# Smaller first loads, last stores on two queues, and a new order of loads and units in a fused attention and GEGLU kernel

## The chip, the cores and the metric

The kernel runs on one core of one Trainium2 chip. The metric is the device time of one execution in microseconds, where lower is better. Times of several executions are given by their median.

## The reference

```python
def _attn_ref(q, k, v):                       # each [8, 12, 448, 64], float32
    S = q.shape[2]
    scale = 1.0 / np.sqrt(q.shape[-1])
    scores = scale * np.matmul(q, k.transpose(0, 1, 3, 2))
    attn = np.maximum(scores, 0.0) ** 2 / S
    return np.matmul(attn, v)

def _moe_ref(x, w_gate, w_val, w_out):        # x [3584, 768]; w_gate, w_val [768, 1536]; w_out [1536, 768]
    g = x @ w_gate
    gelu = 0.5 * g * (1.0 + erf(g / np.sqrt(2)))
    return gelu * (x @ w_val) @ w_out
```

The attention has a squared ReLU in place of the softmax, so there is no sum over a row. Its output, with the heads side by side, is the `x` of the second part. The result is [3584, 768] in float32.

## The kernel before

**Stages.** For each of the eight batches q, k and v come in by DMA from POOL, converted to bf16 on the way. q and k are turned so that the head dimension lies on the partitions: on TensorE for batches 0 and 1 and one third of batch 2 (`add_transposes`, L676), by DMA transposes on SP for the rest (`add_dma_transposes`). A score unit (`add_scores`) makes scores for two heads at a time; ACT applies the ReLU while it empties the PSUM bank (L743), and DVE squares (L752). `add_values` multiplies by v, and the result is `xT`. The gate and value products come either as plain units (`add_gate_value`: a gate or a value for one batch and 128 columns of the 1536) or, for pairs of batches, in a scheme of seven products in place of eight (`add_pair`). Their GELU times value is `uT`. The last product, with w_out, also goes in seven products for a group of four chunks of 64 rows by two tiles (`add_product`); there are 14 groups, 0 to `FINAL` = 13, and each makes two output tiles `osb` of 128 rows. When both column halves of a tile have been read out of PSUM, its two halves of 64 rows are stored with one DMA each.

**The array.** Nearly all matmuls use a quarter of TensorE (64 rows by 64 columns). Two streams, `PE0` for the upper rows and `PE1` for the lower ones, run side by side, each with two column halves.

**The order.** All instructions are put in order before the launch by `run_plan`, which walks a model of the engines with a cost for every step and emits each step when the model starts it. Up to the first gate unit the order of TensorE is fixed by numbers in the code. After that the units stand in a list, written out in `LINE`: a token of one character is the next item of a kind (`s` scores, `o` values, `0` to `7` plain gate or value of that batch), `0E3` is product 3 of the pair of batches 0 and 1 in column block E, and `n2` is product 2 of output group n (13). `next_unit` looks at the first 60 entries and takes the first whose inputs are there. So `LINE` gives preferences. `LOADS` fixes the order of the DMA loads after those of batch 0: `w` one pair of blocks of w_gate and w_val, `o` a part of w_out, `q` a third of the heads of a batch for q and k, `v` the same for v. POOL issues them in that order. A fixed list (`for h0, h1 in ...` before `load_qk`) gives the loads of batch 0.

**Choice of an engine.** A step may carry `other`, a second engine with its own cost and its own emission. It then stands in the pools of both engines, and whichever is free first in the plan takes it. Until now only ACT and DVE steps have such an `other`.

**Cost of a store.** `op.stored` is the time that the plan puts on its one DMA line for a store of 64 rows.

Of the kernel before, what the change touches and what calls it, by code (L numbers as in the profile page):

```python
# [9 lines left out]


LINE = """
0E3 2A4 o s s s s a6 1 0 0 s o o s 3 s 0E1 2C4 b6 1 2A2 5 d5 b2 b5 s 2A6 1 0F5 s 0 c2 o b3 s 0 a2
0E2 2 s 2A3 2F4 s 0 2F1 s d1 s s s 0 o 0 2C2 2E5 0 s s 0 0 1 0E6 o 0 1 2B1 o 0F3 s s s 0F1 s 5 0E7
o 1 2 s o 3 1 1 s 0F7 a1 3 0 0E4 1 s s 0 s 4D1 s 1 0 2B7 1 2C1 2 o s 0F2 b4 s s 1 0E5 2D1 s 0 o s s
2D5 s 0F6 2E1 c6 0F4 2A1 o 5 1 s a7 1 s 0 s s a5 0 s 1 2B4 s s 0 s 1 s 1 a4 1 s o s o 4B3 h1 s s s
1 o 2B2 s 6D5 c3 2D6 2 1 s 2B3 s c1 4 6J5 s c7 s 2A5 b1 2C3 s s a3 f3 2 2E3 2 s 2 s 2F6 3 2E6 2 4D6
b7 2 c5 2B6 s d6 o o 6F1 s 2D7 f1 s s o 4 s o s o 2F3 4 s s 2C6 6B4 e7 c4 4D3 4B4 2F2 e1 2 s s 6D4
4A4 2D2 2B5 s 2A7 3 o 2C7 3 s s d7 s f6 h2 4 5 6K1 4D2 4D7 2D3 s 2E4 h3 2E7 2D4 2E2 s e2 f5 o s 3 s
3 d3 e5 2 2F7 s o 2C5 s 6B7 4C5 g6 s 2 4D4 o 4A2 6H1 s 2F5 4F1 4F2 f7 4B1 4A1 s 4E5 6H4 s f2 e3 d4  # L20
s 3 s l4 m7 6K5 s 3 s o s l6 e6 s s s s s 4F6 s s o o s d2 o s 4C6 3 s g3 s s 3 6A5 s 4 s g1 g2 4F5
i1 f4 6G3 4A5 4 6I1 e4 s h6 4B2 o s o 4C2 g7 6K4 s 4B7 6D3 s 4E1 4A3 i4 4 s g5 s 4 s s 4A6 g4 4B6 s
4F3 4A7 6C5 6C6 s 4C4 s s j3 o 6F6 k7 o s 6F7 s 4C1 s s o 4 s s k1 4 h7 o 4F4 4B5 6B1 j6 4E4 o 4F7
6B2 s s s 6D7 s s 4C7 4E2 4E6 6I7 o 4 s k5 4C3 4D5 s 4 h5 k3 i5 s 5 4E7 6K3 s s j4 s 6D2 s o 6G5 o
j1 5 6E5 5 i3 s 4E3 6A4 s 6D6 j5 6A3 i7 6B6 6G1 s o s 5 5 6B5 s s s j2 s 6D1 5 s 5 s h4 s 5 s i2
6K6 s l5 6L3 6G7 o 6H2 s s 6E6 6C3 m1 i6 6I2 j7 s s k6 s l2 s 6F2 o 6E7 o 6G2 6K2 6I4 6J1 6A1 6A2
n3 m6 6A6 6C1 6B3 6C7 m4 m3 6F5 6A7 6C2 n6 6C4 6H5 6E1 6I5 6L4 6J2 6J3 6E2 6L6 6J6 6H7 n5 6G6 6H3
n4 k4 k2 6L1 m2 6E4 l7 l1 6F4 n1 l3 6L7 6F3 6E3 6J4 n2 6H6 n7 6I6 6J7 6L2 6G4 6L5 m5 6K7 6I3
"""
# [288 lines left out]
def kernel(  # L318
# [97 lines left out]
    ACT, DVE, POOL, GPS, SP, IDLE = [], [], [], [], [], []  # L416
# [12 lines left out]
    def load(nbytes, emit, deps=(), cost=0.7, rate=400e3):  # L429
        def paced():  # L430
            ins = emit()
            for d in op.behind:
                tc.add_manual_dep(ins.ins, d.ins.name, SYNC, reason="pace")
            if turned:
                tc.add_manual_dep(ins.ins, turned[-1].ins.name, SYNC, reason="pace")
            loaded.append(ins)

        op = Op("POOL", cost, paced, deps)
        op.behind = [*deps]
        arrivals[op] = nbytes / rate  # L440
# [20 lines left out]
    def load_qk(b, i, h0, h1, deps=()):  # L461

        src = (q, k)[i]
        m, r0 = divmod(h0, 4)

        def tile_of():
            if (b, m) not in qk16:
                qk16[b, m] = hpool.tile([128, 4, SC * D], bf16, name="qk16", tag="qk16")
            return qk16[b, m][HALF[i], r0:r0 + h1 - h0, :]

        op = load(4 * (h1 - h0) * S * D, lambda: nc.gpsimd.dma_start(  # L471
            tile_of(), src[b, h0:h1].rearrange("h (p c) d -> p h (c d)", c=SC)),
            deps, rate=400e3 if b else 300e3)
        qk_loads.setdefault((b, m), []).append(op)
        for pr in range(h0 // 2, h1 // 2):
            head_op[b, pr, i] = op

    def load_v(b, h0, h1, deps=()):

        m = h0 // 4  # L480
        for i in range(2):
            def emit(i=i):
                if (b, m) not in v16:
                    v16[b, m] = qkv.tile([128, 4, VC, D], bf16, name="v16", tag="v16")
                c0 = i * (SC - VC)
                return nc.gpsimd.dma_start(  # L486
                    v16[b, m][HALF[i], :, :, :],
                    v[b, h0:h1].rearrange("h (p c) d -> p h c d", c=SC)[:, :, c0:c0 + VC, :])
            op = load(4 * (h1 - h0) * VC * P * D, emit, deps, rate=400e3 if b else 300e3)
            v_loads.setdefault((b, m), []).append(op)  # L490
            for pr in range(h0 // 2, h1 // 2):
                head_op[b, pr, 2 + i] = op
# [700 lines left out]
    def add_product(at, gr, name, final):  # L1193
# [76 lines left out]
        engine = "DVE" if added else "ACT"  # L1270
# [12 lines left out]
        def emit_store(j, engine=nc.sync, part=slice(0, d_model)):  # L1283
            b, c = chunks[t % 2][j]
            rows = out[b * S:(b + 1) * S, :].rearrange("(p c) d -> c p d", c=SC)
            engine.dma_start(rows[c, :, part], osb[t][HALF[j], part])

        if name in "2345":
            st["done", t] = [*st.get(("done", t), ()), *reads]
            if final and t == t0:  # L1290
                SP.append(Op("SP", 0.6, lambda: emit_store(0, nc.sync, cols), reads, prio=-1))
                ACT.append(Op("ACT", 0.5, lambda: emit_store(1, nc.scalar, cols), reads, prio=-1))
                SP[-1].stored = ACT[-1].stored = 0.25
            elif len(st["done", t]) == 2:
                queues = (SP, "SP", 0.6, nc.sync), (ACT, "ACT", 0.5, nc.scalar)
                stored[t] = []
                for j in range(2):
                    pool, name_, cost, engine = queues[j if gr >= FINAL - 1 else 0]
                    op = Op(name_, cost, lambda j=j, engine=engine: emit_store(j, engine), st["done", t],
                            lag=2.5, prio=-1)  # L1300
                    op.stored = 0.5
                    stored[t].append(op)
                    pool.append(op)
        for b in {b for tile in (chunks[1:] if "hold" in st else chunks) for b, _ in tile}:
# [7 lines left out]
                    u.grabs = [st["read", "1"], rd]  # L1312


    for h0, h1 in ((0, 2), (2, 4), (4, 8), (8, 12)):
        load_qk(0, 0, h0, h1)
        load_qk(0, 1, h0, h1)
        if h0 == 0:
            POOL.append(Op("POOL", 0.6, lambda: make_identity(nc, ident)))
        if h0 > 2:  # L1320
            load_v(0, h0 - 4, h1 - 4)
    load_v(0, 8, 12)
    late_loads.append(0)
    late = [(b, m) for b in range(2, B) for m in range(NM)]
# [28 lines left out]
    FINAL = B * SC // 4 - 1  # L1353
# [34 lines left out]
    for gr in range(FINAL + 1):  # L1388
        work += [(LATER, 5, add_product, (gr, x, gr == FINAL)) for x in CHAIN]
# [98 lines left out]
    def old_half(b, pr):  # L1488
        return divmod(2 * b + pr // K3 - RING_X, 2)

    for (b, pr), op in x_op.items():
        op.deps += reads_x.get(old_half(b, pr), ())
    for op in [*ACT, *DVE]:
        if op.other is not None:
            {"ACT": ACT, "DVE": DVE, "GPS": GPS}[op.other[0]].append(op)

    for u in later:
        if u.name[0] == "o":
# [56 lines left out]
```

## Time and profile before

| | |
|---|---|
| median of 3 runs | 402.57 us (402.08 to 403.37) |
| the profiled execution | 401.2 us, its span 399.4 us |
| TensorE (PE) busy | 389.7 us, 98% of the span |
| VectorE (DVE) busy | 312.4 us, 78% |
| ScalarE (ACT) busy | 256.7 us, 64% |
| GpSimd (POOL) busy | 97.9 us, 25% |
| mean granted TensorE clock | 0.998 |

The profile is of one execution. Its span goes from the first to the last event on the core; what lies around it is the difference to that execution's own time. Start times count from the beginning of the span. A wait is put down to what ended it. DMA loads are issued from POOL, DMA transposes and most stores from SP, a few stores from ACT.

### The profile page before, as it was taken

The numbers are of one execution on the slowest core, as the hardware profiler recorded it, in microseconds if no ns is written. First come the engines' busy times: TensorE is split into PE (matmuls) and PEld (weight loads), VectorE is DVE, ScalarE is ACT, GpSimd is POOL, SyncE is SP. The second block draws the span as 40 slices with busy tenths as digits, with TensorE's granted clock in tenths as the row PEclk, the third lists the DMA queues.
The fourth block names the chain that finished last, engine by engine and source line by source line (L and its number), as shares of the span: only waits on it lengthen the run. The fifth ranks groups of instructions, "written<-read, shape, count | busy, mean of one in ns | idle before, by whom it ended". The sixth has DMA issues, their size and how long they took to land.

```text
span 399.4 us, 18497 instructions
## 1 busy us (share of the span) xinstructions
PE 389.7 (98%) x8411; PEld 333.4 (83%) x8414; DVE 312.4 (78%) x534; ACT 256.7 (64%) x391; POOL 97.9 (25%) x143
## 2 busy tenths in 40 slices
PE   7999999999999999999999999999999999999994
PEld 3455768888988988888999989888899999988993
DVE  2886799868877688879876878979989897858752
ACT  4867776577687755767767658777878465454210
POOL 7539333060140130132002022040100033444100
PEclk9999999999999999999999999999999999999999
DMA  7999999879696594567589689695512320000137
GB/s 107 173 184 168 197 200 179 119 103 153 84 192 131 92 182 105 92 93 109 62 140 161 95 129 217 98 133 71 84 27 69 100 63 4 3 2 3 24 81 218
DMA packets 75022, 44.38 MB, mean 111 GB/s; under 512 B 34368, under 2 KB 71488, under 8 KB 74944
## 3 DMA queue, kind: packets, MB, share of 16 engines
q0 software_dynamic: 38752, 24.39, 45.2%
q1 hardware_dynamic: 35792, 18.03, 22.7%
q8 instruction: 66, 1.08, 1.1%
q10 hardware_dynamic: 400, 0.79, 0.6%
q14 instruction: 12, 0.10, 0.1%
HBM read 48.76 MB, written 11.01 MB: 150 GB/s over the span
## 4 chain that ended last, share of the span: by engine, by line
PE 94%; DMA 2%; issue 1%; POOL 1%; ACT 1%; DVE 1%; POOLq 0%
PE ff L409 84%; PE sp L409 8%; DMA qk<-in_k_dram 2%; PE sp L676 1%; POOL qk L471 1%; PE ff L597 1%; PE ff L676 1%; ACT attnT L743 0%; DVE part L981 0%; DVE qkr L890 0%; ACT osb L1267 0%; POOL ident masks.py:199 0%; POOL ident masks.py:197 0%; ACT xT L825 0%; POOLq L1539 0%
## 5 line engine op out<-in xcount | busy, mean ns | idle before, releaser
L743 ACT ACTIVATE attnT<-sp 128x896 bf16<-128x896 f32 x168 | 151.4, 921 | 44.4 <-PE sp L409 41.8
L409 PE MATMUL ff<-xT,wg 64*64 64x448 bf16 x1680 | 168.2, 349 | 0.0
L409 PE MATMUL ff<-xT,wv 64*64 64x448 bf16 x1056 | 112.4, 349 | 0.0
L409 PEld LDWEIGHTS <-wv 64*64 64x64 bf16 x1680 | 95.2, 106 | 12.0 <-issue 0.9
L752 DVE TENSOR_TENSOR attnT<-attnT 128x1792 bf16<-128x1792 bf16 (+1 forms) x98 | 92.3, 952 | 13.6 <-ACT attnT L743 13.1
L409 PEld LDWEIGHTS <-wg 64*64 64x64 bf16 x1680 | 92.5, 106 | 10.4 <-issue 0.2
L409 PE MATMUL ff<-attnT,v 64*64 64x448 bf16 (+1 forms) x768 | 81.4, 326 | 0.2
L409 PE MATMUL sp<-qkT 64*64 64x448 bf16 (+1 forms) x768 | 72.7, 328 | 1.3 <-ACT qkT L647 0.6
L409 PE MATMUL ff<-ts,wv 64*64 64x448 bf16 x624 | 70.5, 349 | 0.0
L409 PEld LDWEIGHTS <-s 64*64 64x64 bf16 x1200 | 68.0, 107 | 2.7
L409 PE MATMUL ff<-wt,s 64*64 64x384 bf16 x624 | 55.8, 323 | 0.0
L981 DVE TENSOR_TENSOR part<-ff,part 128x448 f32<-128x448 f32 x78 | 47.1, 620 | 9.5 <-PE ff L409 5.7
L409 PE MATMUL ff<-wo,s 64*64 64x384 bf16 x576 | 53.5, 323 | 0.0
L409 PE MATMUL ff<-ts,ws 64*64 64x448 bf16 x480 | 52.9, 349 | 0.0
L409 PEld LDWEIGHTS <-uT 64*64 64x64 bf16 x912 | 50.7, 107 | 2.6 <-issue 0.6
L486 POOL DMA_DIRECT2D v<-in_v_dram x48 | 29.8, 634 | 84.5 <-ACT attnT L743 44.4
L409 PEld LDWEIGHTS <-v 64*64 64x64 bf16 x768 | 44.4, 107 | 5.6 <-issue 1.6
L409 PE MATMUL ff<-wo,uT 64*64 64x384 bf16 x576 | 48.0, 323 | 0.2 <-issue 0.2
L409 PEld LDWEIGHTS <-ws 64*64 64x64 bf16 x720 | 42.0, 106 | 5.0 <-issue 0.7
L471 POOL DMA_DIRECT2D qk<-in_q_dram x25 | 15.7, 629 | 121.9 <-DMA qkT<-qkr 24.1
L409 PEld LDWEIGHTS <-qkT 64*64 64x64 bf16 x768 | 34.3, 106 | 8.8 <-issue 3.9
L977 ACT COPY part<-ff 128x448 f32<-128x448 f32 x54 | 28.4, 532 | 17.3 <-PE ff L409 16.7
(76 smaller groups left out, 503.8 us busy)
## 6 DMA issues: line engine op xcount, KB each, us to landing
out_dram<-osb SPq DMA_DIRECT2D x51, 192.0 KB, 3.6
v<-in_v_dram POOLq DMA_DIRECT2D x48, 128.0 KB, 6.3
qk<-in_q_dram POOLq DMA_DIRECT2D x23, 224.0 KB, 5.6
qk<-in_k_dram POOLq DMA_DIRECT2D x23, 224.0 KB, 6.1
wg<-in_moe_w_gate_dram POOLq DMA_DIRECT2D x6, 384.0 KB, 8.4
wv<-in_moe_w_val_dram POOLq DMA_DIRECT2D x6, 384.0 KB, 9.6
wo<-in_moe_w_out_dram POOLq DMA_DIRECT2D x8, 288.0 KB, 7.1
out_dram<-osb ACTq DMA_DIRECT2D x3, 192.0 KB, 4.0
```

The source lines that it names most:

```text
L409: return nc.tensor.matmul(o, lhsT, rhs, start=start, stop=stop, skip_group_check=onto, tile_position=(P * row, P * col))
L471: op = load(4 * (h1 - h0) * S * D, lambda: nc.gpsimd.dma_start(tile_of(), src[b, h0:h1].rearrange("h (p c) d -> p h (c d)", c=SC)), deps, ...
L486: return nc.gpsimd.dma_start(v16[b, m][HALF[i], :, :, :], v[b, h0:h1].rearrange("h (p c) d -> p h c d", c=SC)[:, :, c0:c0 + VC, :])
L597: nc.tensor.matmul(t[:, :], warm[:, 0:128], warm[:, :], start=True, stop=True)
L676: nc.tensor.transpose(t[HALF[j], c, :], src[:, 2 * r + j, c, :], ident[:, :], tile_position=(0, P * j))
L743: relu.ins = nc.scalar.activation(duo["a"][:, u % 2, :, :], box[0][:, :, 0:S], AF.Relu).ins
L752: nc.vector.tensor_tensor(a[:, part], a[:, part], a[:, part], op=ALU.mult)
L977: rd.ins = copy(st["t", name][:, :], box[0][:, 0:S]).ins
L981: rd.ins = nc.vector.tensor_tensor(t[:, :], box[0][:, 0:S], t[:, :], op=ALU.add).ins
```

## The change

Four things change. In the loads of batch 0, heads 4 to 7 of q and k come as two loads each, of two heads, in place of one of four; the v loads keep their place behind them. For the output groups from `FINAL - 2` on, each store may be issued from SP or from ACT, whichever is free first in the plan; the first half of a tile is put down for SP and the second for ACT. Before, only the second half of groups from `FINAL - 1` on was on ACT, always, and everything else on SP. The first tile of the last group is stored by column halves, one DMA from SP and one from ACT each; this is as it was. For the same groups the plan counts 0.6 us of DMA time for a store in place of 0.5. `LINE` is another order of the same 558 tokens, and `LOADS` another order of the same 52.

The core of the diff (of `LINE` the first three lines and the last one of each):

```diff
 LINE = """
-0E3 2A4 o s s s s a6 1 0 0 s o o s 3 s 0E1 2C4 b6 1 2A2 5 d5 b2 b5 s 2A6 1 0F5 s 0 c2 o b3 s 0 a2
-0E2 2 s 2A3 2F4 s 0 2F1 s d1 s s s 0 o 0 2C2 2E5 0 s s 0 0 1 0E6 o 0 1 2B1 o 0F3 s s s 0F1 s 5 0E7
-o 1 2 s o 3 1 1 s 0F7 a1 3 0 0E4 1 s s 0 s 4D1 s 1 0 2B7 1 2C1 2 o s 0F2 b4 s s 1 0E5 2D1 s 0 o s s
...
-n4 k4 k2 6L1 m2 6E4 l7 l1 6F4 n1 l3 6L7 6F3 6E3 6J4 n2 6H6 n7 6I6 6J7 6L2 6G4 6L5 m5 6K7 6I3
+a3 1 s 1 s s o s 2D4 0 s 1 o 0 2A1 s 0F5 o o 0 s f1 2 0F6 s s 0E3 2A3 2 0F4 0 o o o 0 0 0F3 o o o
+0F7 s s 2 a4 1 c6 s s 0 s 0F1 s b1 o 5 d1 d4 6C6 2D6 s s s s 0E2 0F2 0 s c1 s s s s 0 0E5 a7 1 1 s
+6F5 2C4 0E1 1 2B1 s 0E7 s 2 0 o 0 0 0E6 1 o 0 1 s 1 f7 s s 0 0E4 4B6 s a1 5 o c4 2 s s s 2F2 b2 s 0
...
+l5 6H2 6I2 m5 6J3 6G6 n5 6F2 6L4 6F3 l2 6J4 6G4 6H4 6I6 6G5 n7 6H7 k2 6L6 6J6 6K5 6I4 n2
 """
 
 LOADS = """
-w q q w q v q w v w w v o v q v q o w q q o o v q v q v v v v q q q q v v q v v q q q q v v q v v
-q v v
+w q q w q v q w v w w v w q v q o v q o q v o o q v v q v v v q q v q v q v q q q v v q q v v q q v
+v v
 """
...
@@ -1295,10 +1295,12 @@
                 queues = (SP, "SP", 0.6, nc.sync), (ACT, "ACT", 0.5, nc.scalar)
                 stored[t] = []
                 for j in range(2):
-                    pool, name_, cost, engine = queues[j if gr >= FINAL - 1 else 0]
+                    (pool, name_, cost, engine), spare = queues[:: -1 if j and gr >= FINAL - 2 else 1]
                     op = Op(name_, cost, lambda j=j, engine=engine: emit_store(j, engine), st["done", t],
                             lag=2.5, prio=-1)
-                    op.stored = 0.5
+                    if gr >= FINAL - 2:
+                        op.other = spare[1], spare[2], lambda j=j, engine=spare[3]: emit_store(j, engine)
+                    op.stored = 0.5 if gr < FINAL - 2 else 0.6
                     stored[t].append(op)
                     pool.append(op)
         for b in {b for tile in (chunks[1:] if "hold" in st else chunks) for b, _ in tile}:
@@ -1312,13 +1314,14 @@
                     u.grabs = [st["read", "1"], rd]
 
 
-    for h0, h1 in ((0, 2), (2, 4), (4, 8), (8, 12)):
+    for h0, h1 in ((0, 2), (2, 4), (4, 6), (6, 8), (8, 12)):
         load_qk(0, 0, h0, h1)
         load_qk(0, 1, h0, h1)
         if h0 == 0:
             POOL.append(Op("POOL", 0.6, lambda: make_identity(nc, ident)))
-        if h0 > 2:
-            load_v(0, h0 - 4, h1 - 4)
+        if h0 == 6:
+            load_v(0, 0, 4)
+    load_v(0, 4, 8)
     load_v(0, 8, 12)
     late_loads.append(0)
     late = [(b, m) for b in range(2, B) for m in range(NM)]
@@ -1490,9 +1493,9 @@
 
     for (b, pr), op in x_op.items():
         op.deps += reads_x.get(old_half(b, pr), ())
-    for op in [*ACT, *DVE]:
+    for op in [*ACT, *DVE, *SP]:
         if op.other is not None:
-            {"ACT": ACT, "DVE": DVE, "GPS": GPS}[op.other[0]].append(op)
+            {"ACT": ACT, "DVE": DVE, "GPS": GPS, "SP": SP}[op.other[0]].append(op)
 
     for u in later:
         if u.name[0] == "o":
```

More of the change, by code (lines that the diff above doesn't have):

```diff
@@ L12 @@
 LINE = """
-0E3 2A4 o s s s s a6 1 0 0 s o o s 3 s 0E1 2C4 b6 1 2A2 5 d5 b2 b5 s 2A6 1 0F5 s 0 c2 o b3 s 0 a2
-0E2 2 s 2A3 2F4 s 0 2F1 s d1 s s s 0 o 0 2C2 2E5 0 s s 0 0 1 0E6 o 0 1 2B1 o 0F3 s s s 0F1 s 5 0E7
-o 1 2 s o 3 1 1 s 0F7 a1 3 0 0E4 1 s s 0 s 4D1 s 1 0 2B7 1 2C1 2 o s 0F2 b4 s s 1 0E5 2D1 s 0 o s s
-2D5 s 0F6 2E1 c6 0F4 2A1 o 5 1 s a7 1 s 0 s s a5 0 s 1 2B4 s s 0 s 1 s 1 a4 1 s o s o 4B3 h1 s s s
-1 o 2B2 s 6D5 c3 2D6 2 1 s 2B3 s c1 4 6J5 s c7 s 2A5 b1 2C3 s s a3 f3 2 2E3 2 s 2 s 2F6 3 2E6 2 4D6
@@ L18 @@
[L18 to L27, printed above, removed]
-n4 k4 k2 6L1 m2 6E4 l7 l1 6F4 n1 l3 6L7 6F3 6E3 6J4 n2 6H6 n7 6I6 6J7 6L2 6G4 6L5 m5 6K7 6I3
+a3 1 s 1 s s o s 2D4 0 s 1 o 0 2A1 s 0F5 o o 0 s f1 2 0F6 s s 0E3 2A3 2 0F4 0 o o o 0 0 0F3 o o o
@@ new lines @@
+0F7 s s 2 a4 1 c6 s s 0 s 0F1 s b1 o 5 d1 d4 6C6 2D6 s s s s 0E2 0F2 0 s c1 s s s s 0 0E5 a7 1 1 s
+6F5 2C4 0E1 1 2B1 s 0E7 s 2 0 o 0 0 0E6 1 o 0 1 s 1 f7 s s 0 0E4 4B6 s a1 5 o c4 2 s s s 2F2 b2 s 0
+a5 a2 s s s o 0 3 b3 2B4 1 1 s s s 4C4 4 0 s 1 2B5 3 s 1 s o s 1 s 2E7 s 0 c3 s k7 s b4 1 a6 2B2 1
+1 6D4 o 1 2A5 2 c7 2D1 o 6A1 2D5 2F1 2 2C3 b7 b5 1 s d6 s s s 3 s 2F3 2B3 b6 2C1 s 4D1 c2 2 s s s
+2A4 s 2E4 4A3 s e1 3 s 2E6 2C2 6D7 c5 2B6 2A2 4F6 f5 2 s 2F6 2D2 s 2B7 s 2A6 s s 2D3 o s 4D7 2 s
+2C6 2D7 2C5 s 2A7 g2 o 3 s 2E1 4C1 2C7 s s 4F1 o d5 4C2 s s 2F4 d7 s s o 4C3 s s 2E2 h1 s 3 o 3 4E5
@@ new lines @@
+g1 3 g6 s e6 o 4A2 4A1 4A5 s s e5 g5 6D1 e2 s 2E3 2F7 s 2F5 2E5 4 4A4 s s 2 3 4D6 i7 s s 6B7 o s 4
+2 4D4 6B1 d2 o o s f2 s e7 3 s s d3 e4 5 s 3 4D3 s s h6 s s o 5 e3 s 3 f3 6J5 s 6I1 4B3 o h5 4 4 f6
+s s m6 s 6F6 g7 s g4 s s 4E1 6G1 4B1 6A3 s o h3 s f4 s 4 4 4B7 m4 s s 4A7 k1 4 s g3 s 4E6 4E3 4B2 s
+n3 4A6 j3 o o 4C5 4 s 6K7 o 4C6 6G7 o j5 s 6A6 4D2 j6 i3 6E4 4B4 i1 s s s 4E2 4B5 s 4D5 s 4F3 6E5 o
+h4 k5 4F7 j1 s 4 s 4F2 4C7 4 6D5 l7 6H5 4 6A2 s 6D3 o 5 s o s s 4F5 o 4E4 s 4F4 6I7 6F7 s s s o 4E7
@@ L29 @@
+6D6 s 6F1 h2 5 6H3 s 5 s s 5 s h7 m2 k3 6J1 5 s s s s 5 6B6 5 s o i6 6B2 6H6 6G2 6E7 o j2 5 i2 s s
+s 6J2 6E1 k6 6B5 s s s i5 j7 i4 s 6K4 l6 6L1 j4 s s 6A7 m3 6B4 k4 o 6A5 6C4 6C7 6F4 6L3 6D2 6B3 6L7
+n1 6E2 6C3 6K1 6C1 6A4 6C2 n6 m1 6E6 l3 n4 6K3 6I5 6J7 6L5 l4 6G3 6C5 6E3 6I3 m7 l1 6L2 6H1 6K6 6K2
+l5 6H2 6I2 m5 6J3 6G6 n5 6F2 6L4 6F3 l2 6J4 6G4 6H4 6I6 6G5 n7 6H7 k2 6L6 6J6 6K5 6I4 n2
 """
 LOADS = """
-w q q w q v q w v w w v o v q v q o w q q o o v q v q v v v v q q q q v v q v v q q q q v v q v v
```

## The prediction

> **What bounds the kernel now.** I read the page first, then the windows by stage, the chain of waits, and last the timelines of the first 54 us and of the end.
>
> ```profile
> span 399.4 us, 18497 instructions
> PE 389.7 (98%) x8411; PEld 333.4 (83%) x8414; DVE 312.4 (78%) x534; ACT 256.7 (64%) x391; POOL 97.9 (25%) x143
> L597 PE MATMUL ff<-held 128*128 128x512 bf16 x15 | 5.0, 397 | 0.2 <-issue 0.2
> 5.60:12.00 6.40, 5.00 (x71) 2.34 (x74) 3.90 (x7) 5.29 (x7) 4.36 (x8) 1.00 1.15 158
> 17.00:26.00 9.00, 8.79 (x134) 5.04 (x135) 8.98 (x17) 9.00 (x11) 2.87 (x4) 1.00 1.33 189
> 26.00:50.00 24.00, 23.84 (x486) 16.06 (x482) 16.97 (x26) 14.86 (x22) 13.80 (x20) 1.00 1.33 182
> 50.00:56.00 6.00, 5.72 (x90) 3.90 (x85) 5.76 (x9) 4.61 (x7) 1.70 (x4) 1.00 1.39 198
> 60.00:160.00 100.00, 99.80 (x2238) 87.54 (x2231) 80.03 (x131) 68.17 (x101) 21.25 (x33) 1.00 0.84 134
> 160.00:260.00 100.00, 100.00 (x2270) 89.18 (x2265) 83.00 (x142) 72.33 (x111) 16.05 (x26) 1.00 0.76 119
> 260.00:360.00 100.00, 99.88 (x2216) 92.39 (x2207) 83.67 (x142) 65.18 (x108) 23.59 (x27) 1.00 0.32 56
> ```
>
> The columns of the windows are length, then busy time and count of PE, PEld, DVE, ACT and POOL, then the granted clock, the DMA share and GB/s. PE is busy 98% of the span, but that number cannot show what is still to be had: an array with one quarter at work counts as busy, and the 15 fillers of L597 (matmuls on a constant tile) count 5.0 us. So I go by the count of matmuls against what the array does at its best.
>
> ```profile
> 4.93 6.70 DMA qk<-in_k_dram
> 71.26 11.26 PE ff L409 x240
> 329.91 63.83 PE ff L409 x1390
> ```
>
> The chain (start, us, what) gives the best rate: 240 matmuls in 11.26 us, 46.9 ns each with 448 columns; near the end, where most have 384 columns, 63.83 us for 1390, 45.9 ns. In 60:360 the windows hold 6724 matmuls, 44.6 ns each, so about the whole of that stretch runs at the array's rate. No order of units shortens it by more than a fraction of a microsecond per hundred. In 50:56 there are 90 matmuls: 90 x 46.9 ns = 4.2 us of work in 6 us, so 1.8 us are lost there though PE shows 5.72 busy. From 5.6 to 26 the counts are lower still, but there ACT sets the pace. What the change can move is therefore the first 60 us and the end.
>
> **The split loads.** Heads 4 to 7 of the first batch come now as one load of q and one of k; afterwards as two each.
>
> ```profile
> 4.32 0.64 POOL L471 DMA_DIRECT2D qk<-in_q_dram  x1
> 4.93 0.64 POOL L471 DMA_DIRECT2D qk<-in_k_dram  x1
> 5.53 1.27 POOL L486 DMA_DIRECT2D v<-in_v_dram  x2
> 8.47 0.61 POOL L471 DMA_DIRECT2D qk<-in_q_dram  x1 [1.67 <-PE ff L676]
> 11.77 0.58 PE L676 MATMUL ff<-ident,qk 128*64 128x128 bf16 x14 [0.67 <-DMA qk<-in_k_dram]
> qk<-in_k_dram POOLq DMA_DIRECT2D x23, 224.0 KB, 6.1
> qk<-in_k_dram POOLq DMA_DIRECT2D x2, 112.0 KB, 3.1
> v<-in_v_dram POOLq DMA_DIRECT2D x48, 128.0 KB, 6.3
> 7.19 4.97 ACT L743 ACTIVATE attnT<-sp 128x896 bf16<-128x896 f32 x6 [0.48 <-PE sp L409]
> 12.71 0.92 ACT L743 ACTIVATE attnT<-sp 128x896 bf16<-128x896 f32 x1 [0.56 <-PE sp L409]
> 14.00 2.59 ACT L743 ACTIVATE attnT<-sp 128x896 bf16<-128x896 f32 x3 [0.37 <-PE sp L409]
> 16.98 9.05 ACT L743 ACTIVATE attnT<-sp 128x896 bf16<-128x896 f32 x11 [0.39 <-DVE xT L814]
> ```
>
> The k of heads 4 to 7 is issued at 4.93 and is waited for until 11.63 (4.93 + 6.70, the chain's row above). PE stands 0.67 us for it before the transposes of the third pair, and because PE runs in order, the score unit behind them is late as well: ACT, which has 21 relus to do for this batch (6 + 1 + 3 + 11), idles 0.56 us at 12.15. The idle 0.37 before 14.00 hangs on the same transposes (their copy to SBUF, then the next scores); the 0.39 before 16.98 waits for a DVE copy of another pair and stays.
>
> The k of heads 4 and 5 keeps its issue at 4.93 and is 112 KB. Landing of such a half took 3.1 us, but with nothing queued ahead; of a whole one, 6.1 us. So it lands between 8.0 and 11.0, and even the late end is before the transposes' turn at 11.1 (11.77 - 0.67). The 0.56 goes in full; of the 0.37 I take a third, as the fillers stand there too. Gain 0.56 + 0.13 = 0.7 us; bounds 0 (both halves land together) and 0.93.
>
> The price is two more issues on POOL, 2 x 0.61 = 1.2 us. The v loads start at 6.75 instead of 5.53 and are issued by 8.02; the next load begins at 8.47, where POOL now idles 1.67 us for PE. So that idle time hides them with 0.45 us to spare, and without it the loads of heads 8 to 11 would be up to 1.2 us later. The v loads, issued up to 1.2 us later, took 6.3 us: the first would come by about 13.1 (6.75 + 6.3), against their first use at 13.59:
>
> ```profile
> 13.59 0.20 PEld L409 LDWEIGHTS <-v 64*64 64x64 bf16 x2
> ```
>
> I put it at nothing, since the bytes queued ahead of them are the same; the bound is 0.7 us of lateness for the second of the two.
>
> The Trainium skill, "DMA: Bandwidth & Descriptors", section "Anatomy of one DMA", gives each such DMA about 2.0 us fixed plus its bytes at 436 GB/s, which would make the whole load only about 0.3 us later than the half and the split worth next to nothing. The trace disagrees: 6.1 against 3.1 us for twice the bytes.
>
> **Load order and unit order.** LINE is a list of preference: `next_unit` takes the first unit on it whose inputs are there.
>
> ```profile
> 37.74 0.83 POOL L449 DMA_DIRECT2D wg<-in_moe_w_gate_dram  x1
> 38.95 0.82 POOL L449 DMA_DIRECT2D wv<-in_moe_w_val_dram  x1 [0.38 <-DMA qk<-in_k_dram]
> 53.29 0.61 POOL L471 DMA_DIRECT2D qk<-in_k_dram  x1 [0.46 <-DMA wv<-in_moe_w_val_dram]
> 50.00:53.90 3.90, 0.00 (x0) 1.00 1.42 198
> 53.90:56.00 2.10, 2.01 (x22) 1.00 1.33 199
> 52.03 5.77 ACT L743 ACTIVATE attnT<-sp 128x896 bf16<-128x896 f32 x7
> ```
>
> The fifth pair of weights, issued at 37.74 and 38.95, lands at about 53.3: a k load waits until then for it. The two windows are the matmuls that read wg: none from 50 to 53.9, then 22. So PE ran out of gate and value units, and batch 1 was not far enough on to give others: its last seven relus run one behind the other from 52.03. That is the 1.8 us hole. The first twelve letters of LOADS are unchanged, so this landing does not move. The thirteenth changes: the sixth pair of weights (2 x 384 KB, 3.9 us at 198 GB/s) goes ahead of the first part of w_out and of some q and v. The next q load then has 768 KB ahead of it in place of 832 (two w_out parts of 288 and two v of 128), so batch 2 is not delayed. POOL issues the same instructions, in another order.
>
> What can fill the hole is LINE. Counting in the two lists, eleven units of kind `0` (gate or value, batch 0) stand before the twentieth `s` (scores) now, and eight afterwards. One is 24 matmuls, 24 x 46.9 ns = 1.1 us. So up to three are kept back for the time when the weights are late, and batch 1's scores come earlier. Bounds: -1.8 us (hole gone) and, if the list only moves the hole, none; below that lies the slower rival. I take a third, -0.6 us, because the pace of the scores hangs on ACT too. The rest of LINE works where PE has no gaps: 0, bounds -0.5 and +0.5.
>
> **The last stores.**
>
> ```profile
> 393.37 0.94 SPq L1286 DMA_DIRECT2D out_dram<-osb  x1
> 393.37 2.34 SPq L1286 DMA_DIRECT2D out_dram<-osb  x3
> 393.76 0.48 ACT L1267 COPY osb<-ff 128x384 f32<-128x384 f32 x1 [6.02 <-PE ff L409]
> 394.27 0.50 ACTq L1286 DMA_DIRECT2D out_dram<-osb  x1
> 394.00:395.00 1.00, 0.00 (x0) 0.00 (x0) 0.00 (x0) 0.24 (x1) 0.00 (x0) 1.00 0.94 317
> 396.00:397.00 1.00, 0.00 (x0) 0.00 (x0) 0.00 (x0) 0.00 (x0) 0.00 (x0) 1.00 0.95 298
> 397.00:398.00 1.00, 0.00 (x0) 0.00 (x0) 0.00 (x0) 0.00 (x0) 0.00 (x0) 1.00 0.40 129
> ACT osb L1267 <- PE ff L409: 21.8, 11, 6.0
> ```
>
> PE's last matmul ends at 393.74 (329.91 + 63.83), ACT copies until 394.24, and 5.2 us of stores follow. SP issues three of them one behind the other, until 395.71, while ACT is done at 394.77. Spread over both queues, four issues (0.94, 0.50 and the like, from 393.37 on) end at about 394.85: 0.86 us earlier. But the DMA engines are full, 0.94 and 0.95, and move about 300 GB/s until after 397; only bytes that leave before 394 help. I take -0.3 for the queues and -0.1 for the order; bounds 0 and, if nothing but the last two halves were left at 394.3, about -1.3. ACT's added issues, 0.5 us each, stand ahead of its copies of the last products, for which PE's banks wait; its 21.8 us of waiting for PE from 360 to 394 hide them. Without that cover, each would cost up to 0.5 us.
>
> The Trainium skill, same page, section "Issuing engines are not separate DMA queues", says that DMAs from several engines run on the same 16 DMA engines, so that a second queue saves only issue time. The full DMA share above agrees; by that rule the -0.3 would be 0.
>
> **Sum.** -0.7 - 0.6 - 0.4 = -1.7 us. The profiled execution took 401.2 us (span 399.4 and 1.8 around it) and would take 399.5; the median of the three runs, 402.57, lies 1.4 above it, and becomes 400.9.
>
> **Rivals.** *Both ends are set by DMA.* The 0.7 us of the head only make the hole at 50 longer, as the weights still land at 53, and the tail stays full: at most the 0.3 is left, 402.3. For it: DMA share 1.33 and more from 17 to 56. Against: batch 1's chain of relus moves forward with the head. Chance 0.22. *The halves land together*, as q, k and v share the engines: no head term, 401.6. Against it: k of 112 KB in 3.1 us. Chance 0.03. *The new order starves PE between 40 and 60*, the slower side. The gate and value units that batch 0 can run before 53 are limited by the weights there; each one that the list spends before it is needed lengthens the hole by 1.1 us. With two the hole grows by 2.3 us and with the tail's 0.4 the time is 404.5; from two on it is slower. Against it: eight instead of eleven. For it: in the list's beginning six `0` stand before the tenth `s`, against three now. Chance 0.20.
>
> **Numbers.** My forecast has 0.55. A change of 0.3%, 1.2 us, is about what a measurement of this kernel can tell from none. Faster by more: 0.55; within it the first two rivals, 0.25; slower 0.20. The range goes from 398.4 (head -0.93, hole -1.8, tail -1.3) to 404.0, which leaves out the worse half of the slower rival.
>
> **What would show it.** Head: no DMA wait before the third pair's transposes, ACT's 21st relu done at 25.3 instead of 26.0. Hole: over 100 matmuls in six microseconds around 50, and wg read in them. Tail: the last issues of SP and ACT within 0.5 us of each other, and less than 5.2 us from the last copy to the end. Wrong: if the 60:360 counts change by over 1%, if a window of 26:60 falls under 15 matmuls per us, or if wv's fifth load lands later than 54.

## The result and the profile after

| | before | after |
|---|---|---|
| median of 6 runs each | 402.72 us (401.49 to 403.37) | 399.28 us (399.09 to 400.35) |
| ratio, 95% interval | | 0.9924 [0.9904, 0.9945] |
| profiled execution, span | 401.2, 399.4 us | 399.09, 397.3 us |

The changed kernel is 0.8% faster. The two profiled executions differ by 2.1 us, the medians by 3.4: the profiled execution of before was shorter than all six of its timed runs (lowest 401.49), that of after was the shortest of its six, 0.2 below their median. So 2.1 us is what these two traces can account for; more traces of both kernels follow. In the longer comparisons below, the kernel before has medians of 402.02, 402.00 and 402.16 us (35, 28 and 23 runs), and after once more has 399.30 us with a ratio of 0.9940. So the six times of before above lie rather high, and the change is worth about 2.4 to 3.1 us (from the ratios 0.9940 and 0.9924).

The page of after, first its span and engines, then one row of its list of DMA issues:

```profile
span 397.3 us, 18514 instructions
PE 388.5 (98%) x8411; PEld 334.7 (84%) x8414; DVE 314.6 (79%) x539; ACT 254.9 (64%) x387; POOL 98.5 (25%) x144
...
qk<-in_k_dram POOLq DMA_DIRECT2D x4, 112.0 KB, 4.4
```

The four small k loads (two before) have a median of 4.4 us from issue to landing, between the 3.1 and the 6.1 that bounded them. It mixes two kinds: the first two took 3.0 and 3.6 us, the two new halves 5.3 us each (issued at 4.89 and 6.06, landed at 10.19 and 11.36). The windows of after, with the columns as before (length, busy and count of PE, PEld, DVE, ACT, POOL, then clock, DMA share, GB/s):

```profile
17.00:26.00 9.00, 8.78 (x132) 5.07 (x132) 8.92 (x17) 8.28 (x11) 2.88 (x4) 1.00 1.36 199
26.00:50.00 24.00, 23.94 (x500) 16.92 (x491) 17.46 (x26) 15.77 (x23) 14.07 (x20) 1.00 1.38 189
50.00:56.00 6.00, 5.62 (x96) 3.56 (x93) 5.83 (x8) 5.45 (x7) 1.22 (x2) 1.00 1.45 199
60.00:160.00 100.00, 99.71 (x2231) 92.69 (x2225) 81.16 (x131) 68.16 (x100) 20.67 (x33) 1.00 0.84 134
160.00:260.00 100.00, 100.00 (x2268) 92.02 (x2263) 83.70 (x143) 71.10 (x109) 17.78 (x29) 1.00 0.72 120
260.00:360.00 100.00, 100.00 (x2220) 85.60 (x2215) 84.81 (x148) 64.62 (x107) 19.62 (x22) 1.00 0.30 53
```

26:50 holds 500 matmuls (before 486), but 50:56, where the hole was, only 96 (before 90): at 46.9 ns that is 4.5 of 6 us, still 1.5 lost. The counts of 60:360 sum to 6719 (before 6724). Counts alone mix units of different width, so for the comparison below I use another figure.

**Array time lost.** Every kernel here runs the same matmuls. I give each 64x64 matmul of 448 columns 47.26 ns, others in proportion to their columns, and each transpose 35 ns, add this up to a point of the trace, and subtract it from the time of that point. A constant that is a little off moves all kernels alike. "PE end" is the last matmul's end, "tail" what follows it up to the end of the span. All numbers in us; "old" and "new" is the order (`LINE` with `LOADS`). The short names are those of the experiments below (`e4` is before once more, `e9` after once more). e5, e8 and e10 are not in the table: their instructions come in other orders.

| kernel | order | lost by 26 | 26:60 | of it 50:56 | 60:360 | 360:PE end | PE end | tail |
|---|---|---|---|---|---|---|---|---|
| before | old | 15.73 | 5.82 | 2.41 | 1.78 | 1.71 | 393.72 | 5.63 |
| e1 | old | 15.40 | 5.15 | 2.17 | 2.68 | 1.69 | 393.61 | 6.30 |
| e2 | old | 15.40 | 5.73 | 2.31 | 2.86 | 1.71 | 394.38 | 6.12 |
| e4 | old | 15.40 | 5.25 | 2.17 | 2.77 | 1.73 | 393.83 | 5.81 |
| after | new | 15.02 | 4.92 | 2.27 | 1.67 | 2.23 | 392.52 | 4.80 |
| e3 | new | 15.02 | 5.20 | 2.32 | 1.62 | 2.29 | 392.82 | 5.54 |
| e6 | new | 14.73 | 4.93 | 2.18 | 2.37 | 2.22 | 392.94 | 5.32 |
| e7 | new | 15.40 | 4.97 | 2.27 | 1.29 | 2.29 | 392.64 | 4.87 |
| e9 | new | 14.83 | 4.93 | 2.32 | 1.52 | 2.31 | 392.27 | 4.83 |
| e11 | new | 15.21 | 4.92 | 2.30 | 0.96 | 2.31 | 392.09 | 5.11 |
| e12 | new | 14.83 | 4.93 | 2.13 | 1.52 | 2.26 | 392.23 | 4.87 |

Means of the seven new rows less those of the four old ones: to 26 us -0.48; 26:60 -0.52; 60:360 -0.96; 360 to PE's end +0.56. The tail of the five kernels with both the new order and the choice of the queue is 1.0 shorter than that of before, e1 and e4. Together about -2.4 us.

The first of these, -0.48, is not shown to be the split's. The column to 26 us follows two things. One is the start of the first relu, which differs between executions of one kernel (7.19 us in before and 6.76 in e4, 7.19 in after and 6.98 in e9) and accounts for 0.1. The other is a wait for the large load, which before and e4 met, and which accounts for the rest. But e3 and e11, with the same large load, did not meet it: e3 has lost 15.02 like after, and e1, with the small loads, 15.40 like e2 with the large one.

### The profile page after: what moved, and what is told of

Read it like the earlier page. It is cut to its first block, busy times and chain, and to the rows that moved or that the text cites. A ratio compares the mean times of both kernels' runs of the same rounds, so it can differ in the third digit from the quotient of the medians.

```text
span 397.3 us, 18514 instructions
## 1 busy us (share of the span) xinstructions
PE 388.5 (98%) x8411; PEld 334.7 (84%) x8414; DVE 314.6 (79%) x539; ACT 254.9 (64%) x387; POOL 98.5 (25%) x144
## 3 DMA queue, kind: packets, MB, share of 16 engines
q8 instruction: 66, 1.08, 1.1%
## 4 chain that ended last, share of the span: by engine, by line
PE 94%; ACT 2%; issue 1%; POOLq 1%; DMA 1%; POOL 1%; DVE 0%
PE ff L409 82%; PE sp L409 8%; ACT attnT L743 1%; PE sp L676 1%; PE ff L597 1%; PE ff L1465 1%; POOLq L1553 1%; DMA out_dram<-osb 1%; POOL uT L990 1%; PE ff L676 1%; PE ff L639 0%; DVE osb L1265 0%; ACT gel L985 0%; ACT qkT L647 0%; ACT osb L1267 0%
## 5 line engine op out<-in xcount | busy, mean ns | idle before, releaser
L409 PE MATMUL ff<-xT,wg 64*64 64x448 bf16 x1680 | 173.2, 349 | 0.0
L409 PE MATMUL ff<-xT,wv 64*64 64x448 bf16 x1056 | 114.1, 349 | 0.0
L409 PEld LDWEIGHTS <-wg 64*64 64x64 bf16 x1680 | 95.1, 106 | 9.8
L409 PE MATMUL ff<-attnT,v 64*64 64x448 bf16 (+1 forms) x768 | 83.2, 326 | 0.1
L409 PE MATMUL sp<-qkT 64*64 64x448 bf16 (+1 forms) x768 | 75.0, 328 | 1.3 <-ACT qkT L647 0.6
L409 PEld LDWEIGHTS <-s 64*64 64x64 bf16 x1200 | 71.5, 107 | 2.1 <-issue 0.2
L409 PEld LDWEIGHTS <-uT 64*64 64x64 bf16 x912 | 54.0, 107 | 3.2 <-POOL uT L990 1.1
L409 PE MATMUL ff<-ts,ws 64*64 64x448 bf16 x480 | 54.4, 349 | 0.0
L409 PE MATMUL ff<-wt,s 64*64 64x384 bf16 x624 | 53.7, 322 | 0.0
L409 PEld LDWEIGHTS <-qkT 64*64 64x64 bf16 x768 | 36.4, 106 | 8.8 <-issue 4.2
```

The source lines that it names most:

```text
L409: return nc.tensor.matmul(o, lhsT, rhs, start=start, stop=stop, skip_group_check=onto, tile_position=(P * row, P * col))
```

## The experiments

Each kernel ran in five rounds beside the kernel before. I state each edit against the kernel that it starts from.

### Each part alone, and before once more

e4_before_again is the kernel before, unchanged. e1_split is before with only the smaller loads:

```diff
-    for h0, h1 in ((0, 2), (2, 4), (4, 8), (8, 12)):
+    for h0, h1 in ((0, 2), (2, 4), (4, 6), (6, 8), (8, 12)):
...
-        if h0 > 2:
-            load_v(0, h0 - 4, h1 - 4)
+        if h0 == 6:
+            load_v(0, 0, 4)
+    load_v(0, 4, 8)
```

> The kernel before once more, unchanged, for a second profile. The profiled execution of before took 401.2 us, less than each of its six timed ones (401.5 to 403.4), and the two profiles differ by only 2.1 us where the medians differ by 3.4. If the profile of before was a lucky one, this execution takes 402 to 403 us and the extra lies in one stretch: either around 50:56, where the weights land (landing times vary with HBM), or in the last stores. If it lies nowhere in particular, it is spread over the whole span. The ratio should be 1.000 within 0.003.

> The kernel before with only the loads of heads 4 to 7 split. Theory A (the three parts act in different stretches and add up): ACT's 21st relu is done about 0.7 us earlier, at 25.3 instead of 26.0, and the time falls by 0.5 to 0.8 us. Theory B (the head's gain only lengthens the hole around 50 us, because the weights land when they land): the relu is as early, but the time changes by less than 0.2 us, and the matmuls counted in 50:56 fall from 90 towards 75. Theory C (the new order carries nearly all): no change in the time, as in B, without saying where it goes.

e2_stores is before with only the choice of the queue for the last stores:

```diff
-                    pool, name_, cost, engine = queues[j if gr >= FINAL - 1 else 0]
+                    (pool, name_, cost, engine), spare = queues[:: -1 if j and gr >= FINAL - 2 else 1]
...
+                    if gr >= FINAL - 2:
+                        op.other = spare[1], spare[2], lambda j=j, engine=spare[3]: emit_store(j, engine)
+                    op.stored = 0.5 if gr < FINAL - 2 else 0.6
...
-    for op in [*ACT, *DVE]:
+    for op in [*ACT, *DVE, *SP]:
```

> The kernel before with only the choice of queue for the last stores and their cost of 0.6 us in the plan. Theory A: from the last matmul to the end 4.8 us instead of 5.6, time lower by 0.3 to 0.8 us. Rival (the DMA engines are full, the queue only saves issue time): below 0.2 us. Theory C: no change, since what shortened the tail after is that fewer stores were left to the end by the new order.

e3_order is before with both lists, `LINE` and `LOADS`, of after.

> The kernel before with only the new LINE and LOADS. Theory A: about 0.9 us gained between 26 and 60, about 0.5 us lost around 370 where a product waits for a multiplication on POOL, tail as before: time lower by 0.3 to 1 us. Theory C: lower by 2 to 3.4 us, nearly as much as the whole change.

| | median us | ratio to before |
|---|---|---|
| e4_before_again | 401.65 | 0.9990 [0.9972, 1.0009] |
| e1_split | 401.61 | 0.9974 [0.9949, 1.0000] |
| e2_stores | 401.49 | 0.9984 [0.9959, 1.0009] |
| e3_order | 400.49 | 0.9957 [0.9934, 0.9981] |

The kernel before, in the same rounds, has a median of 402.02 us. Only the order is clearly worth something alone. Neither the split nor the queues can be told from no change, though the three ratios multiply to 0.9915, about the 0.9924 of the whole change.

What was expected came out only in part. The ratio of e4 is 1 within 0.003, but its profiled execution took 401.5 us, not 402 to 403. In e1 the 21st relu ends at 25.62 us, not at 25.3, and 50:56 holds 91 matmuls, so the hole did not grow; its time decides between none of the theories (0 to 2 us lower). In e2 the tail is 6.12 us, longer than any theory had it. The 1.7 us of e3 (interval 0.8 to 2.7) lie between theory A and theory C.

**Why the split is worth so little.** The timeline of ACT, rows of the score relus (start, length, what, count, and in brackets the idle time before it with its releaser), for e4, in which the wait is there, then for e2, which has the same large loads:

```profile
6.76 4.96 ACT L743 ACTIVATE attnT<-sp 128x896 bf16<-128x896 f32 x6 [0.48 <-PE sp L409]
12.32 0.92 ACT L743 ACTIVATE attnT<-sp 128x896 bf16<-128x896 f32 x1 [0.59 <-PE sp L409]
```

```profile
7.57 5.78 ACT L743 ACTIVATE attnT<-sp 128x896 bf16<-128x896 f32 x7 [0.48 <-PE sp L409]
16.61 9.05 ACT L743 ACTIVATE attnT<-sp 128x896 bf16<-128x896 f32 x11 [0.39 <-PE sp L409]
```

In e4 the seventh relu stands behind an idle 0.59, as in before. In e2 seven run without a break and the last eleven end at 25.66, 18.09 us after the first one started. The timelines of PE tell why, at the transposes of the third pair, first e4, then e2:

```profile
11.38 0.58 PE L676 MATMUL ff<-ident,qk 128*64 128x128 bf16 x14 [0.71 <-DMA qk<-in_k_dram]
```

```profile
11.40 0.58 PE L676 MATMUL ff<-ident,qk 128*64 128x128 bf16 x14
```

The same large load, issued the same way, landed in seven profiles at 11.63, 11.05, 10.73, 11.24, 10.66, 10.88 and 11.04 us (before, e2, e3, e4, e5, e10, e11). PE's turn came at 10.7 to 11.4 (earliest in e4, 11.38 - 0.71), so the load is late in only two of the seven, before and e4. With the wait the 21 relus take 18.84 and 18.88 us from first start to last end; without it 18.09 to 18.34, though the load is whole. With split loads the third pair's k landed between 8.78 and 10.19, at least 0.8 us before its turn in every profile. The split takes a real wait away, but one that a given execution may not have.

**Why the queues alone are worth nothing.** ACT's rows at the end of e2:

```profile
394.04 1.53 ACTq L1286 DMA_DIRECT2D out_dram<-osb  x1
395.61 0.48 ACT L1267 COPY osb<-ff 128x384 f32<-128x384 f32 x1 [7.21 <-issue]
```

In the old order the plan gives two stores to ACT just ahead of its last copy. The first (at 393.06) took 0.50 us to issue, the second, shown here, 1.53. PE ended at 394.38, the copy of its last product started at 395.61, 1.2 us late, and the tail grew to 6.12.

### The two lists apart

e5_line_only is before with the new `LINE` and its old `LOADS`; e10_loads_only has the new `LOADS` and the old `LINE`.

> The kernel before with only the new LINE; LOADS, loads of batch 0 and stores are old. The new LINE with the new LOADS gave 0.9957. If the gain comes from the order of units (more score and value units before the gate units), this one keeps it: 0.994 to 0.998, and 60:360 again loses no more than 1.7 us of PE time. If it comes from the order of loads (sixth weights earlier, w_out later, other order of v and q), it falls to 0.999 or more, and the plan, made for other landing times, shows new gaps after 60 us.

> The kernel before with only the new LOADS. The new LINE with the old LOADS was 3.5% slower, though both together are faster. If list and loads fit each other only as a pair, this one is slower by 1% or more as well, with the loss after 100 us. If the new LINE alone is touchy, the new LOADS cost or gain less than 0.5% with the old LINE.

e5: 415.63 us, ratio 1.0354 [1.0318, 1.0389]. e10: 418.38 us, 1.0397 [1.0365, 1.0428]. Windows of e5, then of e10:

```profile
60.00:100.00 40.00, 40.00 (x869) 37.97 (x865) 32.15 (x52) 27.20 (x42) 8.10 (x12) 1.00 0.95 136
140.00:160.00 20.00, 19.85 (x392) 17.63 (x389) 14.60 (x21) 14.25 (x21) 3.68 (x6) 1.00 0.53 84
300.00:340.00 40.00, 37.62 (x807) 30.77 (x800) 34.17 (x59) 22.50 (x36) 4.88 (x4) 1.00 0.25 62
360.00:380.00 20.00, 18.37 (x326) 13.50 (x320) 14.37 (x27) 8.29 (x16) 7.43 (x7) 0.95 0.01 2
```

```profile
160.00:260.00 100.00, 99.33 (x2144) 86.82 (x2141) 81.75 (x140) 64.94 (x96) 15.94 (x26) 1.00 0.75 119
340.00:360.00 20.00, 19.44 (x386) 14.85 (x383) 16.93 (x25) 10.71 (x22) 8.22 (x7) 1.00 0.01 3
```

Up to 100 us both lose nothing beside the old order: array time lost by 100 is 20.76 in e5 and 20.63 in e10, against 20.8 in e4 and 21.55 already by 60 in before. Then the deficits come: e5 loses 3.4 us in 100:160, 6.0 in 260:340 and 5.1 in 360:380; e10 3.5, then 6.0 in 160:260 and 4.9 in 260:340. Either list, set beside the other's old version, costs 3.5 to 4%; together they gain 0.4%. The effect of the two cannot be added up from parts. For e5 neither branch of what was expected foresaw a loss of this size; e10 came out as the first branch says. Why the lost time arises is not shown: no row of PE's waits in these two traces names a load, and in e5 the longest are for DVE and ACT (1.6, 1.5 and 0.7 us).

### The end

e6_no_stores is after without the choice of the queue (the edit of e2 taken back); the order of instructions on PE is that of after.

> The kernel after without the choice of queue and with 0.5 us per store. Same order of units up to the end. If the two queues shorten the tail: from the last matmul to the end 5.4 to 5.8 us instead of 4.8, and the time is 0.5 to 1 us above the kernel after (ratio to before 0.994 to 0.995). Rival (full DMA engines, only issue time): tail and time as after, within 0.2 us.

e6: 400.13 us, 0.9959 [0.9935, 0.9982]. Its tail is 5.32, just under the 5.4 to 5.8 that were expected if the queues help, and that of e3, which also has the new order and the old stores, 5.54; after, e7, e9, e11 and e12 have 4.80 to 5.11. So of the 1.0 us that the tail lost, the order gives 0.5 and the two queues 0.5. The times agree with this, though the intervals overlap one by one: e3 and e6 have ratios of 0.9957 and 0.9959, the kernels that store the whole result with the choice of the queue (after, e7, e9, e11) 0.9924 to 0.9949.

The last issues are not where the queues help. Those of e6 and e3 end on both engines at about the same time too (394.51 and 394.54 in e6). In e6 the last two stores took 2.8 and 3.0 us to land, in after 2.2 and 2.4. Before that, the two stores of one tile were issued at 389.42 and 389.94 in e6, both on SP, and at 389.00 on SP and 389.01 on ACT in after. So I read the gain as bytes that left 0.5 us sooner, with less still to move at the end.

The end of after, in ACT's timeline, then in windows:

```profile
392.01 1.16 ACTq L1286 DMA_DIRECT2D out_dram<-osb  x1
393.21 0.48 ACT L1267 COPY osb<-ff 128x384 f32<-128x384 f32 x1 [4.24 <-DMA out_dram<-osb]
393.72 0.50 ACTq L1286 DMA_DIRECT2D out_dram<-osb  x1
```

```profile
393.00:394.00 1.00, 0.00 (x0) 0.00 (x0) 0.00 (x0) 0.48 (x1) 0.00 (x0) 1.00 0.90 200
394.00:395.00 1.00, 0.00 (x0) 0.00 (x0) 0.00 (x0) 0.00 (x0) 0.00 (x0) 0.78 0.87 237
395.00:396.00 1.00, 0.00 (x0) 0.00 (x0) 0.00 (x0) 0.00 (x0) 0.00 (x0) 0.50 0.60 163
```

PE ended at 392.52, but the last copy started at 393.21: the store that ACT issued at 392.01 held it for 1.16 us, and the copy stands behind it on the same engine. Does the end hang on that copy, or on bytes? e7_copy_free lets the copy go to DVE; e12_less_bytes leaves out one store of 192 KB, so 64 rows of the result are never written.

```diff
 # e7_copy_free, from after
-        if final and name == "3":
-            rd.other = None
 # e12_less_bytes, from after, in emit_store
+            if (t, j) == (27, 1):
+                return
```

> The kernel after, but the last copy out of PSUM may go to DVE as well as to ACT. In the kernel after, that copy is ready at 392.5 and starts on ACT only at 393.2, behind a store that took 1.16 us to issue there. If ACT's queue is what holds it, the copy starts at 392.6 on DVE, and the end is 0.4 to 0.7 us earlier. If the transfers set the end (DMA share near 0.9 until 395), the copy is earlier but the end moves by less than 0.2 us.

> The kernel after without one of its last stores: the second-last full one on SP, 64 rows of 768, issued at 392.0, is left out, so these 64 rows of the result are never written. If the transfers set the end, 192 KB less at about 300 GB/s end it 0.5 to 0.7 us earlier. If issue and landing of the last two half stores set it (issued at 393.7, 2.6 to 2.9 us to landing), it ends as before, within 0.2 us.

e7: 399.56 us, 0.9949 [0.9930, 0.9968]. e12: 399.1 us, 0.9926 [0.9898, 0.9954]; beside it, on the same chip, e9_after_again: 399.3 us, 0.9940 [0.9916, 0.9964].

> The kernel after once more, for a second profile and a longer comparison. Its first ratio was 0.992; e6 and e7, which differ from it only behind the last product, gave 0.996 and 0.995. If the first six runs were a little lucky, this gives 0.993 to 0.996. In its profile the stretch 60:360 again loses 1.3 to 2.4 us of PE time, against 1.8 to 2.9 with the old order.

DVE's row of e7, and its windows:

```profile
392.67 0.56 DVE L1267 COPY osb<-ff 128x384 f32<-128x384 f32 x1 [0.58 <-PE ff L409]
```

```profile
394.00:395.00 1.00, 0.00 (x0) 0.00 (x0) 0.00 (x0) 0.00 (x0) 0.00 (x0) 1.00 0.91 247
395.00:396.00 1.00, 0.00 (x0) 0.00 (x0) 0.00 (x0) 0.00 (x0) 0.00 (x0) 0.80 0.69 177
```

The copy came 0.54 us earlier, at 392.67, and the last two stores were issued 0.46 and 0.36 earlier, but the span ended at 397.51 against 397.32: the DMA engines were as full (share 0.91 in 394:395), and these stores took 2.9 us to land in place of 2.2 and 2.4. That is the second branch of what was expected. The windows of 392:394 in e12, then in e9:

```profile
392.00:394.00 2.00, 0.23 (x4) 0.00 (x0) 0.00 (x0) 0.48 (x1) 0.00 (x0) 1.00 0.55 137
```

```profile
392.00:394.00 2.00, 0.27 (x4) 0.00 (x0) 0.00 (x0) 0.48 (x1) 0.00 (x0) 1.00 0.86 221
```

With the store left out the DMA share fell from 0.86 to 0.55, and the end, 397.10, is the same in both, again the second branch. Neither cause alone moves the end; both nearly tie. Taking both away at once was not tried. e9 came out as expected: ratio 0.9940, 1.52 us lost in 60:360.

### The wait at 370 us

The waits of after hold two rows that before has not (who waits, on what: sum, number, longest, in us), and one instruction on POOL stands out in its timeline:

```profile
PEld L409 <- POOL uT L990: 1.1, 1, 1.1
PE ff L409 <- POOL uT L990: 0.7, 1, 0.7
```

```profile
368.66 2.58 POOL L990 TENSOR_TENSOR uT<-gel,part 128x448 bf16<-128x448 bf16 x1 [3.29 <-ACT gel L985]
```

The multiplication took 2.58 us where the median of its 18 is 1.04; PE waited for it. The +0.56 of the table after 360 lies there: in 360:380 after loses 1.2 us of array time, before 0.7. DVE's timeline beside it:

```profile
369.86 0.48 DVE L1177 TENSOR_TENSOR s<-s,uT 128x640 bf16<-128x640 bf16 x1
371.27 0.36 DVE L1177 TENSOR_TENSOR qk<-uT 128x128 bf16<-128x128 bf16 x2 [0.93 <-POOL uT L990]
```

When POOL's multiplication starts, at 368.66, DVE is in a run of five bf16 steps of L1177 without a break (from 368.53); the run ends at 370.34, and the multiplication 0.90 us later. All seven profiles of the new order have this, 0.90 us to within 0.01. The reverse is there as well: beside two POOL multiplications that took 1.08 and 1.04 us, from 363.29 on, two steps of L1177 of 128x128 on DVE took 1.06 and 1.34 us, where their like takes 0.21. So the two engines seem to hold each other up; this is read off the traces, and no run tested it. e8_pool_dear makes the plan believe that POOL is slow, so that it would give this step to DVE:

```diff
-                   other=("GPS", 1.05, lambda: emit(nc.gpsimd)) if b >= SPARED else None)
+                   other=("GPS", 2.0, lambda: emit(nc.gpsimd)) if b >= SPARED else None)
```

> The kernel after with 2.0 us instead of 1.05 in the plan for a multiplication on POOL. In the kernel after PE stands about 0.7 us near 370 for one of these that took 2.6 us. If that wait is on the path that sets the end, it goes and the time falls by 0.5 to 1.0 us. Rival: the multiplications go to DVE, which is 79% busy, and products there are late instead: no change, or up to 1 us slower, with DVE as the one that PE waits for between 340 and 380.

e8: 403.04 us, 1.0036 [1.0017, 1.0056], 3.7 us above after, more than either branch allowed. Its profiled execution, 405.19 us, was the slowest of its twelve. The plan did more than move that step: 15 multiplications are left on POOL in place of 18, and from about 330 us on ACT and DVE run their steps in another order. Much of the loss lies there (array time lost from 340 to 380 is 3.1 us, in after 1.4). So the trial tells nothing on the 0.56 itself, which stays a reading of the trace. The long multiplication, 2.57 to 2.58 us, is there in every profile of after, e3, e6, e7, e9, e11 and e12, so the new order brings it.

### After without the split

e11_no_split is after with heads 4 to 7 in one load again.

> The kernel after with the loads of heads 4 to 7 in one piece again. If the split is worth its 0.7 us in every execution: 0.7 us above the kernel after in the same call. What the profiles so far say: in two of four executions without the split PE waited about 0.7 us for that load and in two it had landed 0.1 to 0.3 us before it was needed, so on average 0.3 to 0.4 us above the kernel after, with the wait present or absent in this profile.

e11: 399.77 us, 0.9937 [0.9916, 0.9957], against e9's 0.9940 on the same chip. e3 and e6 are a second such pair, without the choice of the queue: they differ only in the split, and have 0.9957 and 0.9959. On the average the split is worth nothing that can be measured here; the 0.3 to 0.4 us that were expected are smaller than the intervals and are not excluded. The relus of e11 ran without the wait:

```profile
7.41 5.78 ACT L743 ACTIVATE attnT<-sp 128x896 bf16<-128x896 f32 x7 [0.48 <-PE sp L409]
16.46 9.05 ACT L743 ACTIVATE attnT<-sp 128x896 bf16<-128x896 f32 x11 [0.39 <-PE sp L409]
```

None of these kernels is clearly faster than after: the intervals of e7, e11 and e12 overlap its own.

## Why the prediction was right, and where it was not

The forecast was 400.9 us, 1.7 below before; 399.28 came, 3.4 below, within the range. The direction and the size class held, the working only in part. That the sum came out near is partly luck: the head's 0.7 us are not there, and gains that were put at nothing or too low, in 60:360 and in the tail, took its place. The lower end of the range is also added up wrongly: 402.57 - 0.93 - 1.8 - 1.3 is 398.5, not 398.4.

**Head, forecast -0.7: the signs came, but not from the split.** After shows what the prediction asked for:

```profile
7.19 5.78 ACT L743 ACTIVATE attnT<-sp 128x896 bf16<-128x896 f32 x7 [0.48 <-PE sp L409]
13.25 2.59 ACT L743 ACTIVATE attnT<-sp 128x896 bf16<-128x896 f32 x3 [0.29 <-PE sp L409]
16.23 9.05 ACT L743 ACTIVATE attnT<-sp 128x896 bf16<-128x896 f32 x11 [0.39 <-PE sp L409]
```

No wait for the third pair, and the 21st relu ends at 25.28 (forecast 25.3, before 26.0). But e3, with the whole load, ends it at 25.28 too, and e1, with the split, at 25.62. The failed step is that the wait of one profile was taken for a wait of every execution. It was in two of seven, and e1 and e11 show no average gain that can be told from none. The price came out as said: in after the next load is issued at 8.47 as in before, and the first v landed at 12.04, before 13.1. The rule quoted from the Trainium skill, "DMA: Bandwidth & Descriptors", section "Anatomy of one DMA", would have had the split worth next to nothing; that came out for another reason, since small loads did land 0.5 to 2.9 us earlier than whole ones, but the whole one was mostly in time.

**Hole, forecast -0.6: the wrong place.** The matmuls that read wg, in windows of after:

```profile
47.10:52.40 5.30, 0.30 (x4) 1.00 1.45 197
52.40:54.40 2.00, 1.89 (x21) 1.00 1.45 197
```

There were to be over 100 matmuls in six microseconds around 50, and wg read in them. There are 96, and the gap in wg's readers still lasts over 5 us; it only starts 1.4 us earlier than in before, and in e4, the old order again, it starts at 47.5 as well. In the table 50:56 loses 2.1 to 2.4 us in all kernels, in either order. The count of `0` tokens in `LINE` did not tell what the array does there. The gain from 26 to 60 is nevertheless 0.52, near the forecast, but it comes from 40:50 and above all from 56:60, where the old order loses 0.5 us and the new one 0.2. So the right size stands on a wrong reason, by luck.

**60:360, forecast 0 within 0.5 either way: -0.96 by the table.** The profile of before had been the best of the old order there (1.78; e1, e2 and e4 2.68 to 2.86), so "at the array's rate" was read from a lucky execution. The 44.6 ns per matmul was a mean over several widths and could not show the rest. The waits of PE's weight loads in 60:390, of e4 and then of after:

```profile
PEld L409 <- issue: 2.1, 6, 0.5
PEld L409 <- DMA v<-in_v_dram: 0.8, 1, 0.8
```

```profile
PEld L409 <- issue: 1.3, 3, 0.7
```

In three of the four profiles of the old order PE waited for a late v load (0.5 us in e1, 0.2 in e2, 0.8 in e4), in none of the seven of the new order. That is 0.4 us on the average of these four, and it points at the new place of the v loads in `LOADS`, which was put at nothing. The old order also stood more in "issue", the time in which the engine waited for nothing that the profile shows: 1.5 to 2.8 us against 0.5 to 2.0. Before's own trace against after's differs by only 0.1 us in this stretch. One long "issue" stall, near 119 us, follows a packet on the instruction queue that came 9 to 10 us after the one before it, in place of the usual 5 to 6. But after has both as well (0.69 us at 118.5), and e11 has the late packet without the stall. So it does not tell the orders apart: what the stalls are, and why the new order has fewer, is not settled.

**Tail, forecast -0.4: -1.0, under-sized.** The signs came: less than 5.2 us from the last copy to the end (3.6 from its end at 393.69), and the last issues of both queues end together, SP's at 394.18 (the row below) and ACT's at 394.22 (shown above). But the last issues end together in e3 and e6 as well, which have the old stores, so it was the order that took away the three stores one behind the other on SP.

```profile
391.03 3.15 SPq L1286 DMA_DIRECT2D out_dram<-osb  x3
```

Two things were missed. The order brought 0.5 where I had 0.1, and the cover for ACT's added issues failed: I said that ACT's waiting for PE hides them at 0.5 us each, but an issue of 1.16 us held the last copy for 0.69. The rule of the Trainium skill, "DMA: Bandwidth & Descriptors", section "Issuing engines are not separate DMA queues", gave the second queue nothing beyond issue time. Here issue time was worth saving: e6 to after shows 0.5 us with the new order, as an earlier store left sooner. In e2 the gain turns into 1.2 us of a late copy.

**Not in the sum:** the wait for POOL at 370, +0.56.

**The rest of the difference** is the offset. The forecast put 1.4 us between the profiled execution and the median; for after it is 0.2. The three times behind the 402.57 lie high: by the medians of 402.0 to 402.2 in the longer comparisons it would have been about 0.9. The profiles differ by 2.1, not far from the 1.7 of the sum.

**The rivals.** *Both ends are set by DMA* does not hold at the tail, which became 1.0 us shorter; at the head there was no gain that the hole could have swallowed. *The new order starves PE* did not happen: 26:60 lost less than before. In e5 and e10, where `LINE` and `LOADS` do not match, much more is lost from 100 us on, but that units were spent there against late loads is not shown, since PE's waits name no load. The prediction weighed each list by itself, which these two runs show can't be done.

## What to carry to other kernels

A wait of half a microsecond for a load, seen in one profile, may be a race that a given execution wins or loses: look at the landing time in several profiles before it is priced. A sign that is meant to show what one edit does should be looked for in a kernel without that edit too. An order of units and the order of the loads that feed them are one object, and costing the two lists apart says little. A store issued from an engine that also copies the last results stands in that engine's order, so its worst issue time, not the usual one, decides whether it is free.

## What was unexpected of the hardware

- Issuing a store of the same size took 0.47 to 0.50 us in most cases, but 1.06 to 1.53 us for one or two of the last stores in most profiles, on ACT (1.16 in after, 1.46 in e11, 1.53 in e2) and on SP alike (1.28 in e4, 1.52 in e2), with several stores in flight.
- One POOL multiplication took 2.57 to 2.58 us in seven profiles of the new order, the last of its 18, where its like took 1.04; in before the longest took 1.38. It ended 0.90 us after a run of bf16 steps on DVE.
- The same k load, issued at the same place, landed at 10.66 to 11.63 us in different executions, and the first relu started at 6.62 to 7.76 us in executions whose first loads are the same.
